# Position bias of an attention kernel: unit values in 4 bytes instead of 2-byte step tests

## The chip, the core and the metric

The kernel runs on one core of a Trainium2 chip. The metric is the time of one execution in device microseconds (us). The engines named below are TensorE (PE in the profile, its weight loads PEld), VectorE (DVE), ScalarE (ACT), GpSimd (POOL) and the queue of SyncE (SP), which issues most DMAs.

## The reference, cut to what matters

The program is attention with a position bias, then two feed-forward parts with gates. The change touches the bias alone: for each query position i, key position j and head, a network with one input x, 32 hidden units (relu) and 8 outputs.

```python
B, H, S, D = (2, 8, 576, 64); hidden = 32
psi_rel = np.log1p(np.abs(rel))                       # rel = i - j
psi_i = np.log1p(np.maximum(pos[:, None], 1.0))
x = (psi_rel / psi_i)[..., None]
h = np.maximum(x @ w1 + b1, 0.0)                      # w1 (1, 32), b1 (32)
bias = h @ w2                                         # w2 (32, 8)
scores = scores + bias.transpose(2, 0, 1)[None, :, :, :]
...
attn = exp(scores - max) / (sum + 1e-09); out = attn @ v
...
```

## The kernel before, in words

The bias is the same for both batches and depends on i and on the distance |i - j|. It is made once, ahead of the attention, and stored to DRAM (`bias_f`), from where the attention loads it tile by tile.

The work is cut into 36 steps, `g16` = 0 to 35, of 16 query positions each. A step has four *quarters*, c = 0 to 3, of four positions; the 128 partitions of a quarter's tile `s` are four positions x 32 hidden units. Only the longer side of the distances is computed: `width(g16)` columns, 576, 564, 546, ... down to 306 and up again to 576; the other side of the row is a mirror image.

For each step, `gen_s` makes the four tiles `s` (128 partitions x width). An engine makes each: the letters of `TESTS` say which (G GpSimd, A ScalarE, V VectorE). In the kernel before, a tile holds 2-byte tests: 1 or 0 (or a steep sigmoid that is 1 or 0), whether the unit is on at that distance. `bias_mm` multiplies them on TensorE. A weight tile has 32 columns (4 positions x 8 heads), and quarter c writes PSUM partitions 32c to 32c + 31, a quarter of the array's columns. There are two sums, q = 0 (the units' slopes) and q = 1 (their offsets), and each weight is split into two 2-byte parts, p = 0 and 1; the quarter c is the innermost loop:

```python
for q in range(2):
    for p in range(2):
        for sl in sls:
            for c in range(4):
                T.matmul(out=pt[32*c:32*c+32, sl, :], lhsT=wb[p][:, q, :], rhs=s_t[4*g16+c][:, sl, :], ...)
```

VectorE then reads both sums from PSUM: `bias_ev` multiplies the first by 1/psi_i and by the table of psi (tile `t`), `bias_out` adds the second (tile `bo`). `bias_store` has ScalarE write the mirror side (`bo` from `bo`, line 396 or 401) and issues the store on SP, one step late. Ahead of the steps, VectorE works out thresholds from the weights (an exponential by a series) and the split weights; ScalarE converts the first head's q and k (`qs`, `kh`, line 194) once `qk` has landed. Tiles `s` come from a pool of 12. Unit values are made two steps ahead of the step that uses them. GpSimd makes five pieces of the first head's low parts among them (line 192).

Every engine runs its own instructions in program order. After the last step the attention begins: score matmuls (`sc`, line 469), scores plus bias on VectorE (`ng`, line 486), exponentials and so on. Later, line 977 multiplies a 4-byte tile by 4-byte ones (`pc`, 72 columns, eight calls); most other matmuls use tiles declared with a reduced 4-byte type, which the trace calls f32 too.

Of the kernel before, what the change touches and what calls it, by code (L numbers as in the profile page):

```python
# [53 lines left out]
def make_body(stop=None):  # L54
    def body(tc, a):
# [21 lines left out]
        with ctx, tc.manual_schedule():  # L77
# [131 lines left out]
            with ExitStack() as bctx:  # L209
                bc = bctx.enter_context(pool("bc"))  # L210
                sp = bctx.enter_context(pool("sp", bufs=12))
                ev = bctx.enter_context(pool("ev", bufs=2, side="right"))
                pb = [bctx.enter_context(pool("pb", bufs=2, space=PSUM, side=("right", None)[q])) for q in range(2)]
                par = bc.tile([128, 2 + H + 32 + NG4 + 2 * HID + HID * H], F32, name="par")
                rr = bc.tile([128, TW], F16, name="rr")
                tab16 = bc.tile([128, TW + NG16], F32, name="tab16")
# [21 lines left out]
                MAGIC = 1.5 * 2.0 ** 23  # L241
                one = bc.tile([128, 4], F32, name="one")
                sg, kap, dn = one[:, 0:1], one[:, 1:2], one[:, 2:3]
                eu = bc.tile([128, 5, NG4], F32, name="eu")
                v, kf, f, po, pw = (eu[:, i] for i in range(5))
                thr = bc.tile([128, NG4], F32, name="thr")
                nthr = bc.tile([128, NG4], F32, name="nthr")
                rs = bc.tile([128, TW], F16, name="rs")
                big = bc.tile([128, 2 * HID + 1], F32, name="big")
                m1, m2, top = big[:, 0:HID], big[:, HID:2 * HID], big[:, 2 * HID:]  # L250
                sc = bc.tile([128, 2], F32, name="sc")
                ab = bc.tile([128, 2, H], F32, name="ab")
# [929 lines left out]
```

## Time and profile before

| | |
|---|---|
| time, median of 3 runs | 1128.23 us (1128.06 to 1130.68) |
| span of the profiled execution | 1128.2 us |
| TensorE busy | 1093.3 us (97%) |
| VectorE busy | 692.3 us (61%) |
| ScalarE busy | 497.7 us (44%) |
| GpSimd busy | 366.5 us (32%) |

The profile is one execution, whose span runs from its first to its last instruction; of its own time nothing more is shown, and it equals the median of the runs. Shares of busy time are averages over stages with different limits: the bias stage is some 5% of the span, and there the engines stand quite differently from the table.

### The profile page before, as it was taken

Reading aid. Unit: us, or ns where it says so; the run is one execution under the profiler, and the core shown is the slowest. Engines: PE = TensorE matmul, PEld = TensorE weight load, DVE = VectorE, ACT = ScalarE, POOL = GpSimd, SP = SyncE. Lnnn points to the kernel's source line nnn. Section 1 sums busy time; section 2 is a strip of 40 time slices with the busy share of each in tenths; the row PEclk is TensorE's granted clock in tenths of the full one; section 3 lists DMA queues with packets and bytes.
Section 4 is the critical chain, followed back from the end, with each engine's and each line's share of the span. In section 5 each row is a group of like instructions: output and inputs, shape, how many; then the busy total and the mean of one; then the engine's idle time right before and its main releaser. Section 6 shows DMA issues by size and latency. Waiting matters only on the chain.

```text
span 1128.2 us, 18182 instructions
## 1 busy us (share of the span) xinstructions
PE 1093.3 (97%) x7162; PEld 985.8 (87%) x7162; DVE 692.3 (61%) x1214; ACT 497.7 (44%) x903; POOL 366.5 (32%) x258
## 2 busy tenths in 40 slices
PE   6779999999999999999999999999999999999998
PEld 3369898999999989898898988989889898898986
DVE  8989999677735866364554645546455464553633
ACT  7979898433324635152341523415234152341520
POOL 6986997122214402231220312203122031220310
PEclk8899999999999999999999999999999999999999
DMA  5887764133301201020211202112021020110102
GB/s 186 266 243 253 217 188 109 40 114 113 109 20 39 76 19 48 28 75 15 62 47 29 76 11 65 48 28 75 13 63 47 28 76 14 62 48 28 57 19 85
DMA packets 36148, 88.49 MB, mean 78 GB/s; under 512 B 5535, under 2 KB 6494, under 8 KB 35166
## 3 DMA queue, kind: packets, MB, share of 16 engines
q1 hardware_dynamic: 35918, 87.03, 25.4%
q8 instruction: 56, 0.92, 0.3%
q10 hardware_dynamic: 144, 0.29, 0.1%
q14 instruction: 30, 0.25, 0.1%
HBM read 73.24 MB, written 13.28 MB: 77 GB/s over the span
## 4 chain that ended last, share of the span: by engine, by line
PE 76%; DVE 13%; issue 3%; ACT 3%; POOL 2%; DMA 2%; DVEq 0%; SPq 0%; ACTq 0%; POOLq 0%
PE d L1092 35%; PE x L1010 12%; PE y L1010 9%; PE z L1010 8%; PE o L895 3%; PE sc L469 2%; POOL s L343 2%; PE pv L607 2%; DVE ww L106 2%; PE pt L555 1%; DVE ww L111 1%; PE m L658 1%; DVE ng L486 1%; DVE ww L109 1%; PE p L368 1%
## 5 line engine op out<-in xcount | busy, mean ns | idle before, releaser
L1078 POOL TENSOR_TENSOR w2l<-w2r,w2h 128x512 fp32r<-128x512 f32 x64 | 93.6, 1463 | 477.7 <-ACT w2h L1077 469.4
L1106 DVE SCALAR_TENSOR_TENSOR acc<-d,P,acc 128x512 f32<-128x512 f32 x126 | 94.6, 751 | 224.0 <-PE d L1092 223.9
L1092 PE MATMUL d<-w2h,hh 128*128 128x512 f32 x576 | 224.9, 390 | 0.0
L1092 PE MATMUL d<-w2h,hl 128*128 128x512 f32 x576 | 224.6, 390 | 0.0
L1092 PE MATMUL d<-w2l,hh 128*128 128x512 f32 x576 | 224.4, 390 | 0.0
L1018 ACT ACTIVATE s<-x 128x576 f32<-128x576 f32 x96 | 62.5, 651 | 352.8 <-PE x L1010 349.4
L1023 ACT ACTIVATE hh<-s 128x576 fp32r<-128x576 f32 x128 | 87.9, 687 | 93.6 <-DVE s L1035 44.6
L1092 PEld LDWEIGHTS d<-w2h,hl 128*128 128x128 f32 x576 | 108.1, 188 | 23.0 <-DVE hl L1028 0.3
L1092 PEld LDWEIGHTS d<-w2l,hh 128*128 128x128 f32 x576 | 108.2, 188 | 22.0
L1092 PEld LDWEIGHTS d<-w2h,hh 128*128 128x128 f32 x576 | 108.2, 188 | 21.8
L1028 DVE SCALAR_TENSOR_TENSOR hl<-s,hh 128x576 fp32r<-128x576 f32 x128 | 102.1, 815 | 1.8 <-ACT hh L1023 1.5
L835 POOL TENSOR_TENSOR w1l<-wf,w1h 128x768 fp32r<-128x768 f32 x32 | 59.8, 1870 | 77.5 <-ACT w1h L834 67.5
L1010 PE MATMUL x<-xth,w1h 128*128 128x288 f32 x384 | 82.4, 296 | 0.5 <-ACT acc L898 0.5
L1010 PE MATMUL x<-xtl,w1h 128*128 128x288 f32 x384 | 82.2, 296 | 0.0
L1010 PE MATMUL x<-xth,w1l 128*128 128x288 f32 x384 | 82.1, 295 | 0.0
L658 PE MATMUL m<-xh,wh 128*128 128x384 f32 x216 | 73.2, 339 | 2.0 <-DVE t L786 1.9
L658 PE MATMUL m<-xh,wl 128*128 128x384 f32 x216 | 72.8, 337 | 0.7 <-POOL wl L114 0.7
L658 PE MATMUL m<-xl,wh 128*128 128x384 f32 x216 | 72.6, 336 | 0.0
L1044 DVE TENSOR_TENSOR s<-y,s 128x576 f32<-128x576 f32 x32 | 24.2, 757 | 70.4 <-ACT w1h L838 59.4
L1010 PEld LDWEIGHTS x<-xth,w1h 128*128 128x128 f32 x384 | 62.5, 189 | 1.8 <-ACT acc L898 0.7
L1010 PEld LDWEIGHTS x<-xtl,w1h 128*128 128x128 f32 x384 | 61.8, 189 | 0.0
L1010 PEld LDWEIGHTS x<-xth,w1l 128*128 128x128 f32 x384 | 61.8, 189 | 0.0
(194 smaller groups left out, 2463.5 us busy)
## 6 DMA issues: line engine op xcount, KB each, us to landing
wf<-in_moe_w SPq DMA_DIRECT2D x32, 512.0 KB, 3.6
w2r<-in_moe_w SPq DMA_DIRECT2D x64, 256.0 KB, 2.6
bias_f<-bo SPq DMA_DIRECT2D x36, 295.5 KB, 3.4
bias<-bias_f SPq DMA_DIRECT2D x32, 288.0 KB, 3.0
wr<-in_moe_w SPq DMA_DIRECT2D x18, 512.0 KB, 3.7
qk<-in_qk SPq DMA_DIRECT2D x7, 1152.0 KB, 7.3
wr<-in_moe_w_out SPq DMA_DIRECT2D x6, 512.0 KB
vr<-in_v SPq DMA_DIRECT2D x8, 320.0 KB, 6.0
```

The costliest lines, as they stand in the source:

```text
L106: lambda: V.tensor_scalar(out=f, in0=f, scalar1=2.0 ** -15, scalar2=None, op0=ALU.max),
L658: T.matmul(out=p[:, :TG], lhsT=ws[:, 128 * c:128 * c + 128], rhs=xs[:, c, TG * g:TG * g + TG], start=(c == 0 and n == 0), stop=(c == 3 and ...
L835: G.tensor_tensor(out=lo[:, 0:3], in0=t[:, 1:4], in1=raw(hi[:, 0:3]), op=ALU.subtract)
L895: T.matmul(out=p[:, :SH], lhsT=ws[:, 128 * d:128 * d + 128], rhs=xs[:, f, SH * g:SH * g + SH], start=(k == 0), stop=(k == 17))
L1010: T.matmul(out=ps[bank][:, s, :SH], lhsT=ws[:, i, c, :], rhs=xs[:, j, c, s * SH:s * SH + SH], start=(start and k == 0), stop=(k == 5), **kw)
L1018: A.activation(out=t, in_=src, func=AF.Copy)
L1023: A.activation(out=o, in_=src, func=AF.Relu)
L1028: V.scalar_tensor_tensor(out=l, in0=src, scalar=0.0, in1=raw(o), op0=ALU.max, op1=ALU.subtract)
L1044: V.tensor_tensor(out=s2, in0=y, in1=s2, op=ALU.add)
L1078: G.tensor_tensor(out=lo, in0=r, in1=raw(hi), op=ALU.subtract)
L1092: T.matmul(out=pd, lhsT=hs[:, fh, 128 * t:128 * t + 128], rhs=ws, start=(k == 0), stop=(k == 11))
L1106: V.scalar_tensor_tensor(out=acc[:, t, :], in0=pd, scalar=P[:, t, e:e + 1], in1=acc[:, t, :], op0=ALU.mult, op1=ALU.add)
```

## The change

A tile `s` now holds 4-byte values of the units themselves: ScalarE makes relu(slope x psi + b1) with a per-partition scale and bias, GpSimd and VectorE make max(slope x psi, -b1/|w1|), to which a constant is added after the sum (`cv`, one number per output row). psi is read from a 4-byte table. The weights are one 4-byte set (`wf[0]` for ScalarE's tiles, `wf[1]` for the others), so there is one sum and one matmul per quarter, in rounds of at most 512 columns. VectorE reads the sum from PSUM twice: forwards for the computed side, backwards for the mirror side, adding `cv`. ScalarE no longer mirrors. The letters are G, A, V, A in every step. Pools: 14 tiles `s`, 6 tiles `bo`. The thresholds, the series and the weight splitting are gone, as is one input table.

```diff
-TESTS0 = "VVVAAAGG"
-TESTS = "GAVA"
-TESTSL = "GAAA"
+KMAX = 16.0
+TESTS = ("GAVA",)
...
-                sp = bctx.enter_context(pool("sp", bufs=12))
-                ev = bctx.enter_context(pool("ev", bufs=2, side="right"))
+                sp = bctx.enter_context(pool("sp", bufs=14))
+                ev = bctx.enter_context(pool("ev", bufs=6, side="right"))
...
-                par = bc.tile([128, 2 + H + 32 + NG4 + 2 * HID + HID * H], F32, name="par")
-                rr = bc.tile([128, TW], F16, name="rr")
-                tab16 = bc.tile([128, TW + NG16], F32, name="tab16")
+                par = bc.tile([128, 2 + H + 32 + NG4], F32, name="par")
+                tab = bc.tile([128, TW], F32, name="tab")
                 dma(par, a["par"])
-                nc.scalar.dma_start(out=rr, in_=a["tab4"])
-                dma(tab16, a["tab16"])
+                dma(tab, a["tab"])
...
+                ts(sg, w1r, 0.0, ALU.is_ge, 2.0, ALU.mult)
+                ts(sg, sg, -1.0, ALU.add)
+                ts(sl[0], ic4, w1r, ALU.mult)
+                ts(aw, w1r, sg, ALU.mult, 1e-30, ALU.max)
+                ts(sl[1], ic4, sg, ALU.mult)
+                V.reciprocal(out=rec, in_=aw)
+                V.scalar_tensor_tensor(out=wf[0].rearrange("p (i h) -> p i h", h=H),
+                                       in0=w2r.unsqueeze(1).to_broadcast([128, 4, H]), scalar=8.0,
+                                       in1=msk.rearrange("p (i h) -> p i h", h=H), op0=ALU.mult, op1=ALU.mult)
+                ts(nk, b1r, rec, ALU.mult, -1.0, ALU.mult)
+                ts(cb, aw, -KMAX, ALU.mult, b1r, ALU.max)
+                ts(nk, nk, -KMAX, ALU.max, KMAX, ALU.min)
+                ts(wf[1], wf[0], aw, ALU.mult)
...
-                    s = sp.tile([128, 3, 194], F16, tag="s", name="s")[:, :, :n // 3]
-                    win = v3(window(rs, g // 4))
-                    kind = TESTS0[g] if g < len(TESTS0) else (TESTSL if g // 4 == NG16 - 1 else TESTS)[g % 4]
-                    if kind == "A":
-                        A.activation(out=s, in_=win, func=AF.Sigmoid, bias=nthr[:, g:g + 1], scale=STEEP)
+                    s = sp.tile([128, S + 6], F32, tag="s", name="s")
+                    out, win = s[:, :n], window(g // 4)
+                    if kind(g) == "A":
+                        A.activation(out=out, in_=win, func=AF.Relu, bias=b1r, scale=sl[0][:, g:g + 1])
                     else:
-                        eng = G if kind == "G" else V
-                        eng.tensor_scalar(out=s, in0=win, scalar1=thr[:, g:g + 1], scalar2=None, op0=ALU.is_gt)
+                        eng = G if kind(g) == "G" else V
+                        eng.tensor_scalar(out=out, in0=win, scalar1=sl[1][:, g:g + 1], scalar2=nk, op0=ALU.mult, op1=ALU.max)
...
-                    for q in range(2):
-                        pt, sls = sums(pb[q].tile([128, 2, 512], F32, tag="p", name="p"), width(g16))
-                        ps.append(pt)
-                        for p in range(2):
-                            for sl in sls:
-                                for c in range(4):
-                                    T.matmul(out=pt[32 * c:32 * c + 32, sl, :], lhsT=wb[p][:, q, :],
-                                             rhs=s_t[4 * g16 + c][:, sl, :], start=(p == 0), stop=(p == 1))
+                    n = width(g16)
+                    pt = pb[g16 % 2].tile([128, 2, 512], F32, tag="p", name="p").rearrange("p a n -> p (a n)")
+                    for j0 in range(0, n, 512):
+                        js = slice(j0, min(n, j0 + 512))
+                        for c in range(4):
+                            g = 4 * g16 + c
+                            T.matmul(out=pt[32 * c:32 * c + 32, js], lhsT=wf[kind(g) != "A"], rhs=s_t[g][:, js],
+                                     start=True, stop=True)
...
-                    V.scalar_tensor_tensor(out=v3(t), in0=ps[0], scalar=ics[:, g16:g16 + 1], in1=v3(window(l16, g16)),
-                                           op0=ALU.mult, op1=ALU.mult)
...
-                    V.scalar_tensor_tensor(out=v3(bo[:, o:o + n]), in0=ps[1], scalar=sc[:, 1:2], in1=v3(t),
-                                           op0=ALU.mult, op1=ALU.add)
...
-                        A.activation(out=bo[:, 0:z], in_=bo[:, 2 * z:z:-1], func=AF.Copy)
...
+                    for x, y in ((bo[:, at:at + n], pt[:, :n]), (to, src)):
+                        V.tensor_scalar(out=x, in0=y, scalar1=cv, scalar2=None, op0=ALU.add)
...
-                    for n in range(max(g16 - 1, 0), NG16 if g16 == NG16 - 1 else g16):
-                        bias_store(n)
+                    bias_store(g16)
```

TensorE, first step (576 columns), as it stands before: rounds of 2 x 192 and 192 columns, the quarter changing with each matmul; `wb_138` and `wb_139` are the two 2-byte parts of the weights, each matmul with a weight load ahead of it.

```order
L368 LDWEIGHTS wb_138
L368 MATMUL p<-s,wb_138 32x2x192
...
L368 LDWEIGHTS wb_138
L368 MATMUL p<-s,wb_138 32x192
...
L368 LDWEIGHTS wb_139
L368 MATMUL p<-s,wb_139 32x2x192
```

TensorE, the same step after the change: `wf_129` goes with the tiles of GpSimd and VectorE, `wf_128` with ScalarE's.

```order
L297 MATMUL p<-s,wf_129 32x512
L297 MATMUL p<-s,wf_128 32x512
L297 MATMUL p<-s,wf_129 32x512
L297 MATMUL p<-s,wf_128 32x512
L297 MATMUL p<-s,wf_129 32x64
L297 MATMUL p<-s,wf_128 32x64
L297 MATMUL p<-s,wf_129 32x64
L297 MATMUL p<-s,wf_128 32x64
```

Thirty-two matmuls of a step (16 in a step of at most 512 columns) became eight (four), one per quarter and round, each a single row that loads its own weights.

VectorE, steps 0 and 1, as they stand before: `t` and `bo` are the two reads of PSUM, `s` a unit value for a step two further on.

```order
L377 SCALAR_TENSOR_TENSOR t<-p,ics,tab_103 128x576
L343 TENSOR_SCALAR s<-rs,thr 128x3x182
L387 SCALAR_TENSOR_TENSOR bo<-p,sc,t 128x576
L377 SCALAR_TENSOR_TENSOR t<-p,ics,tab_103 128x564
L343 TENSOR_SCALAR s<-rs,thr 128x3x176
L387 SCALAR_TENSOR_TENSOR bo<-p,sc,t 128x564
```

VectorE, the same steps after the change:

```order
L276 TENSOR_SCALAR s<-tab,sl_127,one 128x546
L317 TENSOR_SCALAR bo<-p,cv 128x576
L317 TENSOR_SCALAR bo<-p,cv 128x15
L276 TENSOR_SCALAR s<-tab,sl_127,one 128x528
L317 TENSOR_SCALAR bo<-p,cv 128x564
L317 TENSOR_SCALAR bo<-p,cv 128x31
```

The first read of PSUM is gone, the unit value stands ahead of the step's reads, and the mirror side (15 and 31 columns here) has come to VectorE.

## Rows read from the trace of the kernel before

**Rows 1.** Windows by stretch: busy us of each engine, granted clock, DMA share, GB/s.

```profile
core 0: us, PE busy (x) PEld busy (x) DVE busy (x) ACT busy (x) POOL busy (x), PEclk, DMA share, GB/s
...
12.00:15.00 3.00, 3.00 (x40) 2.10 (x43) 1.76 (x4) 3.00 (x6) 3.00 (x3) 0.50 0.00 0
15.00:45.00 30.00, 23.72 (x398) 9.80 (x391) 29.94 (x63) 27.41 (x62) 29.64 (x24) 1.00 0.79 247
45.00:57.00 12.00, 8.72 (x116) 4.32 (x118) 10.49 (x23) 10.36 (x23) 12.00 (x10) 0.72 0.74 220
...
69.40:73.40 4.00, 3.97 (x17) 3.72 (x18) 3.05 (x7) 1.96 (x5) 3.83 (x3) 0.57 0.76 196
```

**Rows 2.** Chain that ended last, end of the bias stage: start us, us, what.

```profile
63.15 3.42 POOL s L343 x2
...
67.84 0.81 DVE bo L387
...
69.43 4.08 PE sc L469 x16
...
73.64 0.76 DVE ng L486
...
74.81 8.41 DMA bias<-bias_f
```

**Rows 3.** Lines grouped, first 70 us: count | busy us, mean ns | idle before, releaser.

```profile
L343 POOL TENSOR_SCALAR s<-rs,thr 128x564 f16<-128x564 f16 (+17 forms) x36 | 49.3, 1390 | 10.1 <-DVE thr L239 9.9
L340 ACT ACTIVATE s<-rs,nthr 128x576 f16<-128x576 f16 (+17 forms) x72 | 43.1, 650 | 2.0 <-PE p L368 1.6 <-DVE nthr L239 0.3
L368 PE MATMUL p<-s,wb 128*32 128x384 f16 (+21 forms) x736 | 43.0, 341 | 18.8 <-POOL s L343 11.2 <-DVE s L343 6.1 <-DVE bo L387 0.2
L387 DVE SCALAR_TENSOR_TENSOR bo<-p,sc,t 128x576 f32<-128x576 f32 (+17 forms) x36 | 24.2, 671 | 0.7 <-PE p L368 0.4 <-DVE t L377 0.2
L377 DVE SCALAR_TENSOR_TENSOR t<-p,ics,tab 128x576 f32<-128x576 f32 (+17 forms) x36 | 24.1, 670 | 2.7 <-PE p L368 2.7
...
L343 DVE TENSOR_SCALAR s<-rs,thr 128x576 f16<-128x576 f16 (+17 forms) x36 | 15.5, 435 | 0.0
```

**Rows 4.** Timeline of TensorE, one bias step of 546 columns: start us, us.

```profile
16.44 1.11 PE L368 MATMUL p<-s,wb 128*32 128x364 f16 x32 [0.34 <-POOL s L343]
```

**Rows 5.** Timeline of TensorE from 16.44 to 16.46 us.

```profile
16.44 0.34 PE L368 MATMUL p<-s,wb 128*32 128x364 f16 x4 [0.34 <-POOL s L343]
```

**Rows 6.** Timeline of TensorE, a 4-byte product behind others.

```profile
408.18 0.39 PE L1092 MATMUL d<-w2l,hh 128*128 128x512 f32 x1
408.41 0.39 PE L1092 MATMUL d<-w2h,hl 128*128 128x512 f32 x1
408.64 0.34 PE L977 MATMUL pc<-P,ones 128*128 128x72 f32 x2
```

**Rows 7.** Instructions of line 977 alone: ns min/median/max, first and last start.

```profile
L977 PE MATMUL pc<-P,ones x16: 223/248/273, 408.6 to 429.7; 128*128 128x72 f32 x16
```

**Rows 8.** Lines by shape, whole span: count | busy us, mean ns | idle before.

```profile
L1018 ACT ACTIVATE s<-x 128x576 f32<-128x576 f32 x96 | 62.5, 651 | 352.8 <-PE x L1010 349.4
...
L64 POOL TENSOR_SCALAR xh<-x 128x576 fp32r<-128x576 f32 x6 | 4.0, 675 | 0.5
...
L340 ACT ACTIVATE s<-rs,nthr 128x576 f16<-128x576 f16 x4 | 2.9, 765 | 0.3 <-DVE nthr L239 0.3
```

**Rows 9.** Timeline of ScalarE ahead of the bias stage.

```profile
8.99 1.16 ACT L194 ACTIVATE qs<-qk 128x1152 fp32r<-128x1152 f32 x1 [4.70 <-DMA qk<-in_qk]
10.06 1.15 ACT L194 ACTIVATE kh<-qk 128x1152 fp32r<-128x1152 f32 x1
```

**Rows 10.** Timeline of VectorE: end of its preparation, and the last step's `t`.

```profile
11.21 0.29 DVE L239 TENSOR_SCALAR nthr<-eu,one 128x144 f32<-128x144 f32 x1
...
68.57 0.81 DVE L377 SCALAR_TENSOR_TENSOR t<-p,ics,tab 128x576 f32<-128x576 f32 x1
```

**Rows 11.** DMA rate from 0 to 15 us, in 40 slices.

```profile
GB/s 0 0 0 0 54 76 79 257 375 418 429 424 418 454 510 393 418 418 418 418 548 270 396 294 55 0 0 0 0 0 0 0 0 0 0 0 0 0 0 0
```

More of the change, by code (lines that the diff above doesn't have):

```diff
@@ L239, in ts @@
                     V.tensor_scalar(out=out, in0=in0, scalar1=s1, scalar2=s2, op0=o0, **kw)
[L241 to L252, printed above, removed]
-                wf = bc.tile([128, 2, 32], F32, name="wf")
-                wb = [bc.tile([128, 2, 32], F16, name=f"wb{p}") for p in range(2)]
-                ics = bc.tile([128, NG16], F32, name="ics")
@@ L299, in body @@
-                weights += [lambda q=q: V.tensor_tensor(
-                    out=wf[:, q, :].rearrange("p (i h) -> p i h", h=H),
-                    in0=ab[:, q, :].unsqueeze(1).to_broadcast([128, 4, H]),
-                    in1=msk.rearrange("p (i h) -> p i h", h=H), op=ALU.mult) for q in range(2)]
-                weights += [
-                    lambda: V.tensor_copy(out=wb[0], in_=wf),
-                    lambda: V.tensor_tensor(out=wb[1], in0=wf, in1=wb[0], op=ALU.subtract),
-                    lambda: ts(ics, ic16, sc[:, 1:2], ALU.mult)]
@@ L308, in body @@
-                weights.insert(10, lambda: ts(pw.bitcast(I32), kf, 127.0, ALU.add, 2.0 ** 23, ALU.mult))
-                for n in range(max(len(knots), len(weights))):
-                    for steps in (knots, weights):
-                        if n < len(steps):
-                            steps[n]()
-                    if n == 4:
-                        ts(rs, rr, sg, ALU.mult)
+                one = bc.tile([128, 8], F32, name="one")
+                sg, aw, rec, nk, cb = (one[:, i:i + 1] for i in range(5))
@@ new lines, in body @@
+                sl = [bc.tile([128, NG4], F32, name=f"sl{i}") for i in range(2)]
+                wf = [bc.tile([128, 32], F32, name=f"wf{i}") for i in range(2)]
+                cv = bc.tile([128, 1], F32, name="cv")
+                V.memset(cv, 0.0)
+                ts(sg, w1r, 0.0, ALU.is_ge, 2.0, ALU.mult)
[3 more added lines that the diff above has]
+                ts(sl[1], ic4, sg, ALU.mult)
@@ L351, in body @@
                     gen_s(g)
[L353 to L369 removed]
+                for c in range(4):
+                    T.matmul(out=p0[32 * c:32 * c + 32, 0, 0:1], lhsT=wf[0], rhs=cb, start=True, stop=True)
@@ new lines, in body @@
+                for c in (0, 2):
+                    V.tensor_copy(out=cv[32 * c:32 * c + 32], in_=p0[32 * c:32 * c + 32, 0, 0:1])
+                def bias_mm(g16):
+                    n = width(g16)
+                    pt = pb[g16 % 2].tile([128, 2, 512], F32, tag="p", name="p").rearrange("p a n -> p (a n)")
+                    for j0 in range(0, n, 512):
+                        js = slice(j0, min(n, j0 + 512))
+                        for c in range(4):
+                            g = 4 * g16 + c
+                            T.matmul(out=pt[32 * c:32 * c + 32, js], lhsT=wf[kind(g) != "A"], rhs=s_t[g][:, js],
+                                     start=True, stop=True)
@@ L381, in body @@
[L381 to L402 removed]
+                    i0 = 16 * g16
@@ L408, in body @@
[L408 removed]
+                    pt = bias_mm(g16)
                     for c in range(4):
```

106 lines of the change are left out of this document (22 added, 84 removed).

## The prediction, made before the changed kernel ran

> **What bounds the kernel now.** I read the windows by stretch first, then the chain that ended last, then the grouped lines of the bias stage, then single TensorE rows. In the windows [rows 1] the reader is to see that the position bias fills the time from 12 to about 69.4 us, with GpSimd busy 12.0 of 12.0 us in its worst stretch and VectorE 29.9 of 30.0 in its longest, while TensorE has gaps: its granted clock stands at 0.50 (1.2 GHz) when the stage starts, rises to 1.00 (2.4 GHz), and averages 0.72 between 45 and 57 us and 0.57 just after the stage. The chain [rows 2] ends the stage with GpSimd's unit values (line 343), one short TensorE piece, VectorE's sum into `bo`, and the first score matmul at 69.43; from there it goes through `ng` at 73.64 and a bias load of 8.41 us. Everything later is a TensorE-bound program that the change doesn't touch, so what counts is when the first score matmul and the first `ng` start. The grouped lines [rows 3] give the load of the 36 steps: GpSimd 49.3 us of unit values, ScalarE 43.1 us of unit values, VectorE 24.1 + 24.2 us of evacuation and 15.5 us of unit values.
>
> **The change, part by part.** Widths n of the 36 steps go 576, 564, 546, 528, 516, 498, ... 306 and back up; their sum is 15912, their mean 442.
>
> *GpSimd.* The same 36 unit values, now 4 bytes in and out, two operations. The nearest row is a 4-byte two-operation copy of 576 columns at 0.675 us [rows 8]; the 2-byte test of 564 columns is the longest form behind the mean of 1.390 [rows 3]. From below 36 x 0.56 = 20 us (0.675 less 134 columns at 0.86 ns, the slope of a line through a small fixed cost), from above the 49.3 us it costs now. I take 20, since type and kind of the copy are those of the new operation. Hidden in either case unless TensorE's part below comes out under 50 us.
>
> *ScalarE.* 72 Relu in place of 72 Sigmoid, at one element rate; each gets a second per-partition operand. An ACTIVATE without one took 0.651 us at 576 columns, the present one with one 0.765 [rows 8], so a second is worth 0 to 0.11 us: 43.1 + 72 x (0 to 0.11) = 43 to 51 us, taken as 47. The mirror copies leave it.
>
> *VectorE.* `t` goes (24.1 us). `bo` stays at the same price per column, since its operand is still PSUM (24.2 us), and a mirror piece of 15 to 287 columns, 151 on average, comes in: 36 x (0.2 + 151 x 1.06 ns) = 13 us, rate and fixed cost from the present sums (0.81 us at 576 columns, mean 0.670 at 442 [rows 3, 10]). Unit values 15.5 us, or up to 24 at the rate of the sums. Together 53 to 61 us against 63.8 now, all of these durations, of which neighbours overlap a little. Under TensorE's part, and in step with it.
>
> *The prelude.* VectorE's preparation (some 40 operations; the last starts at 11.21 [rows 10]) becomes 12 small ones, so GpSimd and VectorE can start near 6.5 instead of 11.4. ScalarE can't: it first makes the two head copies, which waited for `qk` until 8.99 [rows 9]. The input is smaller by 0.47 MB of the 2.29 MB that land up to then (`rr` gone, `par` 93 instead of 253 KB); at the 0.42 MB/us at which the queues ran [rows 11] that is 1.1 us. Copies from 7.9 to 10.1, the first Relu done at about 11.0. Before, TensorE's first bias matmul stood at 11.98.
>
> *TensorE.* This is the step on which the forecast rests. Now, 2-byte operands: at n = 546 the 32 matmuls of a step took 1.11 us [rows 4]. Each column quarter sees 2 x 2 x 546 = 2184 columns, 0.91 us at 2.4 GHz, plus the tail of the last one, so all four quarters run at once; a stretch of 20 ns holds the starts of four, and no fifth, which would go to the first quarter again [rows 5]. After: one 4-byte matmul per quarter. The only true 4-byte products in the trace are `pc` (72 columns): eight calls left sixteen matmul records [rows 7], so each is two passes. Two passes from 408.64 to their end took 0.34 us [rows 6]; the second took 0.273 [rows 7], so it began 0.06 to 0.07 us after the first: 72 columns at two clocks each (0.06 us). The neighbouring `d` rows move 512 columns in 0.23 us, one clock each. So a quarter needs 4n clocks in two passes, as many as the 2-byte form's 4n in four passes.
>
> But the order of the passes differs. In the old order the quarter changes with every matmul. In the new one both passes of a quarter stand back to back, and the second can't start while the first occupies the same quarter. If TensorE starts matmuls in program order, then the next quarter's first pass starts only together with this quarter's second: two quarters at a time, not four. A step with n up to 512 costs 4 x 2n clocks = 3.33n ns. For n above 512 the code makes a round of 512 columns over four quarters and then a round of n - 512; the short round hides behind the last long pass, but that pass no longer covers the next step's first: 5 x 0.427 + 2(n - 512)/2.4 ns = 2.14 to 2.19 us. Sum: the 26 steps up to 498 (10452 columns) 34.8 us, the ten wide ones 21.6 us, 56.4 us. That is longer than ScalarE's 47, and makes TensorE the bound of the stage.
>
> The Trainium skill says in "TensorE: Matmul & The Clock Gate", Part 3 (What overlaps and what doesn't), that matmuls start and end strictly in program order. By that rule the step costs what I have just worked out; no row here has two passes on one quarter followed by another quarter, so the trace doesn't show it.
>
> *Sum.* 11.0 (first unit of ScalarE) + 56.4 + 0.8 (some 165 passes in series, 5 ns between them, an estimate from the 0.06 to 0.07 above) + 1.6 (the clock stood at 0.50 for about 3.2 us from the first bias matmul [rows 1], half of which is lost) = 69.8 for the last bias matmul and the first score matmul behind it, against 69.43: +0.4. The first `ng` waits for VectorE too, which has the last `bo` (0.81) and its mirror (0.2) to make after TensorE's last pass and its tail (0.16, a `pc` pass of 0.223 us less its 72 columns): 1.2 us, where it now starts about a quarter of the 4.08 us of score matmuls behind the first. That adds 0.2. Coming back: without gaps TensorE should enter the scores at full clock. Now those sixteen matmuls ran at a mean clock of 0.57 and the chain goes through them to the fourth `ng` [rows 1, 2]; four `ng` of 0.76 behind each other are then the longer part, and some 0.5 us are won. Net 0 to +0.6 us. The profiled execution's span is 1128.2 us and the runs' median 1128.23, so no correction is needed: 1128.7.
>
> **The rivals.**
>
> *Four quarters at once* (faster). If the two passes of different quarters interleave freely, TensorE needs 4n clocks a step, 27 us in all, and ScalarE sets the pace: 10.1 + 47 + 0.7 (the value copy) = 58, first score at 59, 10.4 us earlier: about 1118. For it: the 2-byte rows show four quarters at once. Against it: they are in an order that asks for nothing else. The Trainium skill's table in the same page ("Why this matters for your kernels") promises concurrency for small outputs on separate column groups without a word on operand size. By that advice this rival holds.
>
> *One quarter at a time* (slower). If 4-byte passes on different quarters don't overlap at all, a step takes 8 x 2n clocks = 6.67n ns, 106 us in all, the first score comes near 119 and the kernel at 1178. It decides from the first step. Nothing in the trace shows 4-byte passes on two quarters together; nothing speaks against it but that 2-byte ones do.
>
> *Two quarters at the low clock* (slower). If TensorE isn't given 1.00 with half its columns working, 56 us become 113: 1183. Against it: between 15 and 45 us it kept 1.00 although it was busy only 23.7 of 30 us with tails counted [rows 1].
>
> *The new unit values don't get cheaper on GpSimd.* 49 us plus its 10 us of head pieces from 6.5 on ends at 66, a few steps late behind the pieces: 1131 or 1132, within the likeliest case's range.
>
> **How the numbers follow.** Two quarters at full clock 0.70, four 0.10, one 0.10, low clock 0.08, something else 0.02. The likeliest gives 1128.7; its own range is 1125 to 1133: 1.5 us either way for the start of ScalarE and the clock, up to 2.6 us if 20 ns instead of 5 lie between passes, 3 if GpSimd stays dear. What a measurement tells from no change here is 0.3%, 3.4 us. Inside the likeliest case 0.50 is no change, 0.07 faster, 0.13 slower. Faster: 0.10 + 0.07 = 0.17; same 0.50; slower 0.13 + 0.10 + 0.08 + 0.02 = 0.33. The two slow cases are 0.18 together and stay outside the range; the four-quarter case is taken in: 1117 to 1134.
>
> **What would show it.** Right: in the profile after, TensorE without gaps from about 11 to 70 us; two matmul records per quarter; starts of passes of 512 columns 0.43 us apart in pairs; 2.1 to 2.2 us per step at the wide end and 1.0 at 306; GpSimd at 0.55 us per unit value and waiting for buffers; clock 1.00 at the first score matmul. Wrong: starts within some 10 ns for four quarters, and a stage that ends near 58 with ScalarE full; or steps of 3.8 us at 576 and a stage that ends near 119; or a clock of 0.50 through the stage. If ScalarE's Relu took over 0.9 us at 576, or GpSimd over 1.7, one of them would be the bound instead of TensorE.

## The result, and the profile after

The changed kernel takes 1142.04 us, median of four runs (1139.98 to 1143.22), against 1128.24 (1128.06 to 1130.68) for the kernel before: ratio 1.0113, 95% interval 1.0099 to 1.0128. It is 13.8 us slower, outside the range of 1117 to 1134. The profiled execution's span is 1141.4 us, 13.2 more than that of the kernel before; it is the longest of the four runs.

The windows by stretch of the changed kernel, for the stretches of [rows 1] and the 4 us behind its bias stage:

```profile
core 0: us, PE busy (x) PEld busy (x) DVE busy (x) ACT busy (x) POOL busy (x), PEclk, DMA share, GB/s
12.00:15.00 3.00, 3.00 (x24) 1.46 (x24) 0.53 (x1) 3.00 (x5) 3.00 (x2) 0.50 0.00 0
15.00:45.00 30.00, 20.67 (x166) 4.85 (x162) 25.61 (x54) 23.94 (x38) 29.62 (x19) 0.76 0.76 231
45.00:57.00 12.00, 8.45 (x56) 1.23 (x52) 8.10 (x18) 7.66 (x12) 12.00 (x8) 0.57 0.59 165
80.90:84.90 4.00, 3.50 (x31) 3.12 (x24) 3.59 (x9) 1.73 (x5) 3.92 (x3) 1.00 0.70 176
```

GpSimd is the full engine now, 29.6 of 30 and 12.0 of 12 us, and VectorE, which had 29.94 of 30 [rows 1], has room. TensorE is busy less than before, and its granted clock is lower, 0.76 between 15 and 45 us, where it was 1.00. The lines grouped over the first 84 us (count | busy us, mean ns | idle before, releaser) say what it waits for:

```profile
L276 POOL TENSOR_SCALAR s<-tab,sl,one 128x576 f32<-128x576 f32 (+17 forms) x36 | 68.1, 1901 | 4.5 <-DMA tab<-in_tab 4.3
L273 ACT ACTIVATE s<-tab,par,sl 128x576 f32<-128x576 f32 (+17 forms) x72 | 49.2, 746 | 14.9 <-PE p L297 14.9
L297 PE MATMUL p<-s,wf 128*32 128x512 f32 (+18 forms) x368 | 48.4, 608 | 26.3 <-POOL s L276 24.6 <-ACT s L273 1.2
L317 DVE TENSOR_SCALAR bo<-p,cv 128x576 f32<-128x576 f32 (+17 forms) x72 | 34.5, 521 | 21.5 <-PE p L297 21.5
L276 DVE TENSOR_SCALAR s<-tab,sl,one 128x576 f32<-128x576 f32 (+17 forms) x36 | 23.9, 666 | 1.4 <-DMA tab<-in_tab 1.4
```

These answer to [rows 3]. TensorE waits 24.6 us for GpSimd's unit values. The 36 of them take 68.1 us, 1.90 us each, where the tests took 1.39 [rows 3] and the forecast was 0.55. By shape:

```profile
L276 POOL TENSOR_SCALAR s<-tab,sl,one 128x576 f32<-128x576 f32 x2 | 5.0, 2514 | 4.3 <-DMA tab<-in_tab 4.3
...
L273 ACT ACTIVATE s<-tab,par,sl 128x576 f32<-128x576 f32 x4 | 3.3, 856 | 0.5 <-PE p L297 0.5
```

The chain that ended last (start us, us, what), from the last head piece to the first wait for a bias load, answers to [rows 2]:

```profile
57.86 1.39 POOL kl L190
59.25 10.91 POOL s L276 x6
...
73.09 6.69 POOL s L276 x3
...
79.82 1.22 PE p L297 x16
...
81.80 0.24 DVE bo L317
...
82.06 3.40 DMA bias_f<-bo
...
86.10 9.20 DMA bias<-bias_f
```

The end of the stage is GpSimd's, with TensorE's sixteen passes behind it. GpSimd's own timeline has no gap over 0.1 us from its first unit value to its last; the first and the last row of unit values:

```profile
5.77 28.27 POOL L276 TENSOR_SCALAR s<-tab,sl,one 128x576 f32<-128x576 f32 x14 [4.29 <-DMA tab<-in_tab]
...
59.23 20.54 POOL L276 TENSOR_SCALAR s<-tab,sl,one 128x432 f32<-128x432 f32 x10
```

From 5.77 us on, 68.1 us of unit values and four head pieces of 1.4 us (the last is `kl` at 57.86) add up to 79.5; the last value ends at 79.77. The first score matmul stands at 80.93 instead of 69.43 [rows 2], 11.5 us later. The bias load behind it starts 11.3 us later than the one in [rows 2] and takes 9.20 instead of 8.41 us. Line 977 of the kernel before, now line 895, starts at 422.4 instead of 408.6 [rows 7], 13.8 us later, so the whole loss lies ahead of it:

```profile
L895 PE MATMUL pc<-P,ones x16: 223/248/273, 422.4 to 443.4; 128*128 128x72 f32 x16
```

Of the 13.8 us, 12.1 are there when that load has landed (95.30 against 83.22); the other 1.7 fall between there and line 895, and I have not followed them.

The timeline of TensorE (start us, us, idle before) holds the second surprise. The first two rows are the same step of 480 columns, up to 21.46 us and up to 21.90 us; the others are the last step and the first three scores:

```profile
21.43 0.61 PE L297 MATMUL p<-s,wf 128*32 128x480 f32 x4 [0.90 <-POOL s L276]
...
21.43 1.02 PE L297 MATMUL p<-s,wf 128*32 128x480 f32 x8 [0.90 <-POOL s L276]
...
79.82 1.18 PE L297 MATMUL p<-s,wf 128*32 128x512 f32 x16 [1.10 <-POOL s L276]
80.93 0.40 PE L387 MATMUL sc<-kh,qs 128*128 128x288 f32 x1
81.17 0.29 PE L387 MATMUL sc<-kl,qs 128*128 128x288 f32 x1
81.30 0.29 PE L387 MATMUL sc<-kh,qs 128*128 128x288 f32 x1
```

A 4-byte matmul is two passes (two records each, as in [rows 7]), so the step has eight. Four of them start within 30 ns; the other four start after 21.46 and before 21.90 (a pass of 480 columns at two clocks each takes 0.40 us), and all eight are done in 1.02 us with the tail. The forecast's order, two at a time, gives 1.6 us and the tail. So four run at once, which I take for the first passes of the four quarters. The last step, 576 columns, took 1.18 us; 2.19 were forecast.

### The profile page after: what moved, and what is told of

It reads as the page before. It is cut to its first block, busy times and chain, and to the rows that moved or that the text cites. A ratio compares the mean times of both kernels' runs of the same rounds, so it can differ in the third digit from the quotient of the medians.

```text
span 1141.4 us, 17296 instructions
## 1 busy us (share of the span) xinstructions
PE 1098.8 (96%) x6802; PEld 976.0 (86%) x6802; DVE 685.3 (60%) x1187; ACT 493.5 (43%) x864; POOL 384.7 (34%) x258
## 4 chain that ended last, share of the span: by engine, by line
PE 74%; DVE 12%; POOL 5%; issue 3%; ACT 3%; DMA 2%; SPq 0%; DVEq 0%; ACTq 0%; POOLq 0%
PE d L1010 34%; PE x L928 12%; PE y L928 8%; PE z L928 8%; POOL s L276 4%; PE o L813 3%; PE sc L387 2%; PE pv L525 2%; DVE ww L104 2%; PE pt L473 2%; DVE ww L109 1%; PE m L576 1%; DVE ng L404 1%; DVE ww L107 1%; DVE ptl L487 1%
## 5 line engine op out<-in xcount | busy, mean ns | idle before, releaser
L297 PE MATMUL p<-s,wf 128*32 128x512 f32 (+18 forms) x368 | 48.4, 608 | 26.3 <-POOL s L276 24.6
L276 POOL TENSOR_SCALAR s<-tab,sl,one 128x576 f32<-128x576 f32 (+17 forms) x36 | 68.1, 1901 | 4.5 <-DMA tab<-in_tab 4.3
L297 PEld LDWEIGHTS p<-s,wf 128*32 128x32 f32 x368 | 11.0, 125 | 63.6 <-POOL s L276 54.3
```

Of the source, the lines that this page charges most:

```text
L276: eng.tensor_scalar(out=out, in0=win, scalar1=sl[1][:, g:g + 1], scalar2=nk, op0=ALU.mult, op1=ALU.max)
L297: T.matmul(out=pt[32 * c:32 * c + 32, js], lhsT=wf[kind(g) != "A"], rhs=s_t[g][:, js], start=True, stop=True)
```

## The experiments

**The theories.** B, as the expectations call it: GpSimd is the bound because of max. A comparing operation is dear there, a multiplication or an addition isn't. Against it stood the second per-partition operand of the new operation (A), VectorE's work beside it (C), and the 4 bytes. e4, e7, e8, e11 and e12 make the whole computation; the others leave out or change the part named. All kernels but e6 start from the changed kernel, some by way of e7; the kernel before ran beside them on the same chip (1128.35 for the first four, 1128.55 for the next four, 1128.60 and 1129.11 for the last). "First score" is the start of the first score matmul. e2 to e6, e9 and e10 ran once each, so their times have no interval, and the argument goes by the durations in their traces.

| run | GpSimd's 36 (or fewer) operations | mean us | first score | time us |
|---|---|---|---|---|
| kernel before | 2-byte is_gt | 1.39 | 69.43 | 1128.24 |
| changed kernel | 4-byte mult, max | 1.90 | 80.93 | 1142.04 |
| e1 | 4-byte mult, mult | 0.73 | 64.85 | 1124.04 |
| e2 | mult, max with a constant | 1.83 | 78.19 | 1136.66 |
| e3 | mult, add | 0.81 | 65.45 | 1125.70 |
| e4 | mult, max; VectorE makes none | 1.84 | 82.01 | 1140.00 |
| e5 | 4-byte is_gt alone | 1.50 | 67.23 | 1128.54 |
| e6 | the kernel before, 2-byte mult, mult | 0.63 | 69.10 | 1128.07 |
| e9 | 4-byte max alone | 1.50 | 67.86 | 1128.34 |
| e7 | none (mirror copies) | | 66.00 | 1124.64 |
| e8 | 18 mult, max (and mirror copies) | 1.95 | 72.66 | 1132.69 |
| e11 | 9 mult, max (and mirror copies) | 1.88 | 69.54 | 1129.68 |
| e12 | 9 mult, max, issued earlier (and mirror copies) | 2.06 | 62.20 | 1120.86 |
| e10 | none (mirror copies); 140 of 144 unit values left out | | 52.96 | 1112.64 |

**e1: no max on GpSimd.** The maximum is left out on GpSimd's quarter.

```diff
-eng = G if kind(g) == "G" else V
-eng.tensor_scalar(out=out, in0=win, scalar1=sl[1][:, g:g + 1], scalar2=nk, op0=ALU.mult, op1=ALU.max)
+if kind(g) == "G":
+    G.tensor_scalar(out=out, in0=win, scalar1=sl[1][:, g:g + 1], scalar2=1.0, op0=ALU.mult, op1=ALU.mult)
+else:
+    V.tensor_scalar(out=out, in0=win, scalar1=sl[1][:, g:g + 1], scalar2=nk, op0=ALU.mult, op1=ALU.max)
```

> GpSimd's 36 unit values are made as slope x psi x 1.0 (one per-partition operand, one constant); the max with the knee is left out on GpSimd alone, all else is as in the change. This is the form whose price the prediction used. If the price hangs on the operation (either theory, the second operand or the max), GpSimd's unit values fall from 68.1 us to 20 to 25 us (0.56 to 0.7 each, as the copies of this width), TensorE waits for something else, and the stage ends where ScalarE (49 us from 10.7) or VectorE (58 us) ends: first score matmul at 61 to 70 us instead of 80.9, time 1120 to 1129. If it is VectorE's use of the shared memory path, the form hardly matters: GpSimd stays over 55 us and the time near 1138 to 1142.

Measured: 1124.04 us (1121.93 to 1125.38, 6 runs), ratio to the kernel before 0.9957 (0.9945 to 0.9970). Lines over the first 84 us, and the window from 30 to 45 us:

```profile
L299 PE MATMUL p<-s,wf 128*32 128x512 f32 (+16 forms) x368 | 42.4, 482 | 15.4 <-DVE s L278 11.2 <-ACT s L273 3.7
...
L276 POOL TENSOR_SCALAR s<-tab,sl 128x576 f32<-128x576 f32 (+17 forms) x36 | 26.2, 730 | 23.6 <-PE p L299 19.3 <-DMA tab<-in_tab 4.0
L278 DVE TENSOR_SCALAR s<-tab,sl,one 128x576 f32<-128x576 f32 (+17 forms) x36 | 24.4, 681 | 1.2 <-DMA tab<-in_tab 1.1
```

```profile
30.00:45.00 15.00, 9.01 (x86) 2.68 (x86) 15.00 (x32) 14.52 (x25) 11.49 (x14) 1.00 0.85 266
```

GpSimd falls from 68.1 to 26.2 us and now waits for TensorE. The stage ends 16.1 us earlier, and VectorE, busy 15.00 of 15 us, is the bound: TensorE waits 11.2 us for VectorE's unit values. The two multiplications, at 26.2 us, are a little over the 20 to 25 expected and near the 20 of the forecast; what is left to 68.1 goes with max or with the second per-partition operand, which this edit takes out together.

**e2 and e3: the second per-partition operand apart from max.** In e2 max compares with a constant, in e3 the operand stays and is added, on GpSimd's quarter alone.

```diff
+    G.tensor_scalar(..., scalar2=0.0, op0=ALU.mult, op1=ALU.max)   # e2
+    G.tensor_scalar(..., scalar2=nk, op0=ALU.mult, op1=ALU.add)    # e3
```

> GpSimd's unit values are max(slope x psi, 0.0): the knee as a constant in place of the per-partition one, which changes the bias of those units. Theory A, the second per-partition operand is dear: falls to 20 to 30 us in all, as in the mult-mult kernel. Theory B, the max is dear: stays at 60 to 68 us (1.7 to 1.9 each). Theory C, VectorE's traffic: stays at 60 to 68 as well, but then the mult-mult kernel does too.

> GpSimd's unit values are slope x psi + knee: both operands per partition, but an add in place of the max, so no relu on those units. Theory A, the second per-partition operand is dear: stays at 60 to 68 us. Theory B, the max is dear: falls to 20 to 30 us. Theory C: stays.

Measured, the same line in either:

```profile
L276 POOL TENSOR_SCALAR s<-tab,sl 128x576 f32<-128x576 f32 (+17 forms) x36 | 65.3, 1830 | 4.4 <-DMA tab<-in_tab 4.3
```

```profile
L276 POOL TENSOR_SCALAR s<-tab,sl,one 128x576 f32<-128x576 f32 (+17 forms) x36 | 29.1, 810 | 21.3 <-PE p L299 16.8 <-DMA tab<-in_tab 4.2
```

Max with a constant is as dear as with an operand (1.83 against 1.90), and an addition with that operand costs 0.08 us more than a multiplication with a constant (0.81 against 0.73). The rival of the operand (A) falls: 0.07 or 0.08 us of the 1.90 are its share.

**e4: VectorE makes no unit values.** ScalarE makes three of four; the whole computation.

```diff
-TESTS = ("GAVA",)
+TESTS = ("GAAA",)
```

> VectorE's quarter is made by ScalarE (letters G, A, A, A); same results. VectorE then reads PSUM alone and makes no unit values from SBUF, so nothing of its fast reads from SBUF meets GpSimd. Theory C, VectorE's traffic makes GpSimd slow: GpSimd's 36 values fall from 1.90 us each to about 1.0 or less. Theories A and B, the form is dear by itself: they stay at 1.7 to 1.9 (only the long ones, such as 2.75 us for the first of 576 columns beside three VectorE values, come down to the straight line through the others, 2.3). ScalarE becomes the bound: 108 values, 74 us from 10.7, stage end near 86.

Measured, lines over 84 us:

```profile
L276 POOL TENSOR_SCALAR s<-tab,sl,one 128x576 f32<-128x576 f32 (+17 forms) x36 | 65.8, 1837 | 5.1 <-DMA tab<-in_tab 4.1 <-ACT s L273 0.6 <-PE p L297 0.2
...
L273 ACT ACTIVATE s<-tab,par,sl 128x576 f32<-128x576 f32 (+17 forms) x108 | 70.0, 749 | 0.0
```

GpSimd's values take 1.84 instead of 1.90 us: VectorE's unit values beside it are worth 3%. VectorE's sums, which read PSUM, still ran; in e1 both stood beside GpSimd, and its operations took 0.73 us, so C falls. ScalarE, at 70.0 us of work, is full as well (15.00 of 15 us between 30 and 45 us), so the time itself tells nothing.

**e5, e6 and e9: bytes and operation crossed.** e5 keeps only a compare on GpSimd's quarter, e9 only the maximum; e6 is the kernel before with a multiplication in place of its 2-byte test.

```diff
+    G.tensor_scalar(out=out, in0=win, scalar1=sl[1][:, g:g + 1], scalar2=None, op0=ALU.is_gt)   # e5
+    G.tensor_scalar(out=out, in0=win, scalar1=nk, scalar2=None, op0=ALU.max)                    # e9
+    G.tensor_scalar(out=s, in0=win, scalar1=sg, scalar2=1.0, op0=ALU.mult, op1=ALU.mult)        # e6
```

> GpSimd's 36 operations are a single is_gt against one per-partition value, 4 bytes in and out (slope and clamp are left out on GpSimd's quarter; the rest is the kernel after). Theory B (comparing operations are dear on GpSimd, multiplying and adding ones are not, whatever the bytes): as dear as the 2-byte test of the kernel before or dearer, 1.4 to 1.9 us mean, the first score matmul at 70 to 80 us and the kernel at 1129 to 1142. Rival (only max is dear, and the test of the kernel before was slow because of its 2 bytes): 0.7 to 0.8 us mean, first score matmul near 65, kernel near 1124.

> GpSimd's 36 operations are a single max with one per-partition value (the multiplication by the slope is left out on GpSimd's quarter; the rest is the kernel after). A multiplication alone in 4 bytes took GpSimd 0.73 us as a pair of two factors. If the two operations of one instruction cost the sum of their own prices, max alone is 1.90 less 0.4 to 0.7: 1.2 to 1.5 us mean, as the lone compare's 1.50, the first score matmul near 67, the kernel near 1128.5. If the price of max is paid once for the instruction whatever stands beside it, 1.8 to 1.9 us, and the kernel stays at 1137 to 1142.

> The kernel before, with GpSimd's 36 2-byte tests replaced by a 2-byte multiplication of two factors (the test is left out on GpSimd's tiles; all else as before). Theory B: 0.7 to 0.9 us mean instead of 1.39, 25 to 32 us in all; the stage is then set by VectorE (63.8 us of work from 6 to 12 us on, 29.9 of 30 us busy before), so the first score matmul comes 0 to 3 us earlier than 69.4 and the kernel is at 1125 to 1128. Rival (bytes make it slow): 1.3 to 1.4 us mean, and nothing changes: 1128.

Measured, GpSimd's line in e5, e9 and e6, and a window of e6:

```profile
L276 POOL TENSOR_SCALAR s<-tab,sl 128x576 f32<-128x576 f32 (+17 forms) x36 | 53.4, 1498 | 5.3 <-DMA tab<-in_tab 3.7 <-PE p L299 1.4
```

```profile
L276 POOL TENSOR_SCALAR s<-tab,one 128x576 f32<-128x576 f32 (+17 forms) x36 | 53.3, 1496 | 6.0 <-DMA tab<-in_tab 4.0 <-PE p L299 1.7
```

```profile
L343 POOL TENSOR_SCALAR s<-rs,one 128x564 f16<-128x564 f16 (+17 forms) x36 | 22.7, 634 | 33.1 <-PE p L370 19.6 <-DVE t L379 7.6 <-DVE rs L239 5.1
```

```profile
30.00:45.00 15.00, 14.29 (x184) 3.79 (x185) 15.00 (x35) 14.46 (x34) 10.51 (x15) 1.00 0.88 282
```

A lone compare and a lone maximum cost the same in 4 bytes, 1.50 us; the compare in 2 bytes cost 1.39 [rows 3]; multiplications cost 0.73 in 4 bytes and 0.63 in 2. The operation decides, the bytes count for some 10%. The prices look as if they add up: 1.50 for max leaves 1.90 - 1.50 = 0.40 for the multiplication ahead of it, about half of 0.73 for two; a lone multiplication was not run. The price of e5 came as theory B had it, but the time didn't: its first score was expected at 70 to 80 us and stands at 67.23. In e6 GpSimd's load is more than halved, to 22.7 us (25 to 32 were expected), and the kernel stays at 1128.07, against 1128.55 beside it: in the kernel before, GpSimd alone was not the bound, although it stood in the chain at the end of the stage [rows 2]. VectorE is full in that window of e6, 15.00 of 15 us, with ScalarE at 14.46 and TensorE at 14.29 close to it.

**e10: TensorE by itself.** From e7 (below); only the first step's four unit values are made, and all steps multiply those.

```diff
-for g in range(8):
+for g in range(4):
     gen_s(g)
...
-    T.matmul(..., rhs=s_t[g][:, js], start=True, stop=True)
+    T.matmul(..., rhs=s_t[c][:, js], start=True, stop=True)
...
-    for c in range(4):
-        if g16 + 2 < NG16:
-            gen_s(4 * (g16 + 2) + c)
```

> The kernel of the run without a max on GpSimd, in which only the first step's four unit values are made; all 36 steps multiply those (the other 140 unit values are left out). TensorE then waits for no value, only for the sum buffers, which VectorE frees in 24 us in all. Two quarters at a time in program order, as forecast: 2.1 to 2.2 us for a step of 516 to 576 columns, 1.0 us for one of 306, 56 us for all steps from about 11.5 on, the last near 68. Four quarters at once: 0.95 to 1.1 us for a wide step, 0.55 to 0.65 for one of 306, 27 to 32 us in all at 2.4 GHz, the last step near 40 to 45.

Measured: weight loads on TensorE come in fours, one for each quarter, two fours to a step. The timeline of the loads of the steps of 468 (two fours), 450 (two) and 432 columns (the first four, in a row with what follows), at full clock, and the lines of TensorE and VectorE:

```profile
19.35 0.19 PEld L297 LDWEIGHTS p<-s,wf 128*32 128x32 f32 x4 [0.21 <-issue]
19.75 0.20 PEld L297 LDWEIGHTS p<-s,wf 128*32 128x32 f32 x4 [0.20 <-DVE bo L317]
20.14 0.20 PEld L297 LDWEIGHTS p<-s,wf 128*32 128x32 f32 x4 [0.19 <-issue]
20.52 0.22 PEld L297 LDWEIGHTS p<-s,wf 128*32 128x32 f32 x4 [0.17 <-DVE bo L317]
20.89 0.97 PEld L297 LDWEIGHTS p<-s,wf 128*32 128x32 f32 x12 [0.16 <-issue]
```

```profile
L297 PE MATMUL p<-s,wf 128*32 128x512 f32 (+18 forms) x368 | 35.8, 525 | 9.2 <-DVE bo L317 5.8 <-ACT s L273 3.4
L317 DVE TENSOR_SCALAR bo<-p,cv 128x576 f32<-128x576 f32 (+17 forms) x36 | 24.4, 678 | 24.1 <-DMA bias_f<-bo 12.1 <-PE p L297 10.0 <-POOL bo L62 0.5
```

From 19.35 to 20.14 the step of 468 columns takes 0.79 us, from there to 20.89 that of 450 takes 0.75: 4n clocks at 2.4 GHz are 0.78 and 0.75 us. Four quarters at once, without a remainder. So TensorE needs about 27 us for the 15912 columns at 2.4 GHz, not 56. The last step was expected near 40 to 45, but from 24 us on VectorE waits 12.1 us for stores to free `bo`, and the first score stands at 52.96: with nearly no unit values made, the stores hold the stage there.

**e7: a version without max on GpSimd.** The whole computation. VectorE makes two of four unit values, and GpSimd copies the mirror side from the finished `bo`.

```diff
-TESTS = ("GAVA",)
+TESTS = ("VAVA",)
...
+def msrc(bo, m, n, up_):
+    return bo[:, 2 * m:m:-1] if up_ else bo[:, n - 2:n - 2 - m:-1]
...
-for x, y in ((bo[:, at:at + n], pt[:, :n]), (to, src)):
-    V.tensor_scalar(out=x, in0=y, scalar1=cv, scalar2=None, op0=ALU.add)
+V.tensor_scalar(out=bo[:, at:at + n], in0=pt[:, :n], scalar1=cv, scalar2=None, op0=ALU.add)
+pool_copy(to, msrc(bo, m, n, side(g16)[1]))
```

> The whole computation: GpSimd makes no unit values, VectorE makes two of four, and GpSimd makes the mirror piece of the sum by a 4-byte copy from the finished part. GpSimd: 36 copies of 151 columns on average at 0.2 to 0.35 us, 7 to 13 us, no max. VectorE: 36 sums at 0.67 us, 24 us, and 72 unit values at 0.35 us (the short ones of the kernel after) to 0.68 us (its mean beside GpSimd), 25 to 49 us: 49 to 73 us from 5.7 on. ScalarE: 72 Relu at 0.68 us, 49 us from 10.6 on. Theory B with VectorE little disturbed: the stage ends by ScalarE or VectorE at 58 to 64, first score matmul at 60 to 66 instead of 80.9, kernel at 1119 to 1125, faster than both. Rival (VectorE's unit values stay at 0.68 us even without GpSimd's): VectorE ends near 78, kernel near 1138.

Measured: 1124.64 us (1123.84 to 1125.15, 4 runs), ratio 0.9963 (0.9948 to 0.9977).

```profile
L276 DVE TENSOR_SCALAR s<-tab,sl,one 128x576 f32<-128x576 f32 (+17 forms) x72 | 36.9, 556 | 1.3 <-DMA tab<-in_tab 1.3
L319 DVE TENSOR_SCALAR bo<-p,cv 128x576 f32<-128x576 f32 (+17 forms) x36 | 23.8, 666 | 5.5 <-PE p L297 5.3
L62 POOL TENSOR_SCALAR bo<-bo 128x15 f32<-128x15 f32 (+17 forms) x36 | 17.7, 492 | 41.9 <-DVE bo L319 40.9 <-ACT s L273 0.8
```

The upper end of what was expected: VectorE has 60.7 us, unit values at 0.56 us. The 36 mirror copies cost GpSimd 0.49 us each, more than the 0.2 to 0.35 expected, but GpSimd waits 40.9 us for VectorE's sums ahead of them. 17.4 us of the changed kernel are gone.

**e8, e11, e12: some max on GpSimd.** The whole computation, from e7. GpSimd makes one value in every second step (e8), in every fourth (e11), or in every fourth but issued four steps ahead of its use instead of two, with 16 tiles `s` instead of 14 (e12). In e11 and e12 alike the values are issued at steps 1, 5, 9 and so on up to 29, and the head pieces at others; only one value of the nine is placed differently, at step 33 for the last step in e11, ahead of the first step in e12.

```diff
+TESTS = ("GAVA", "VAVA")                   # e8
+TESTS = ("VAVA", "VAVA", "VAVA", "GAVA")   # e11
+TESTS = ("VAVA", "GAVA", "VAVA", "VAVA")   # e12
...
+sp = bctx.enter_context(pool("sp", bufs=16))                     # e12
...
-        if g16 + 2 < NG16:
+        if g16 + 2 < NG16 and kind(4 * (g16 + 2) + c) != "G":    # e12
             gen_s(4 * (g16 + 2) + c)
+    if g16 + 4 < NG16 and kind(4 * (g16 + 4)) == "G":
+        gen_s(4 * (g16 + 4))
```

> The whole computation, as the run beside it, but GpSimd makes its unit value (with max) in every second step: 18 values at 1.85 us, 33 us, plus 7 to 13 us of mirror copies and about 10 us of head pieces: 50 to 56 us from 5.7 on, so it ends at 56 to 62. VectorE: 36 sums, 24 us, and 54 unit values at 0.35 to 0.68 us, 19 to 37 us: 43 to 61 us. ScalarE as in the kernel after, 49 us from 10.6 on, ends at 60. If the price of a max is all that made the kernel after slow, all three end near 60 and the first score matmul is at 60 to 64: 1119 to 1123. If GpSimd's long operations hold up its mirror copies, which the stores wait for, the gain is less: 64 to 72, 1123 to 1131.

> The whole computation; as the run without a max on GpSimd, but in every fourth step GpSimd makes one unit value: 9 values at 1.9 us, issued two steps before a head piece and two after, so that each has two steps of about 1.5 us. VectorE has 9 unit values of 0.56 us less: 55.7 us instead of 60.7, and it was busy all the time from 15 to 60 us. If GpSimd's long operations fit between the pieces, the first score matmul comes 2 to 5 us earlier than 66.0, at 61 to 64, the kernel at 1120 to 1123. If TensorE again waits for GpSimd, as with a max in every second step, it comes at 66 to 69: 1124 to 1128.

> The whole computation; GpSimd makes one unit value with a max in every fourth step, as in the run before, but issues it four steps ahead of its use instead of two, at a step that has no head piece and not for the wide last step (a pool of 16 tiles s instead of 14). If TensorE's waits of 2 us for each of the nine values came from GpSimd's queue (the value stands behind a mirror copy, which waits for the sum of the step before), they go, VectorE keeps its 5 us of relief, and the first score matmul comes at 61 to 65 instead of 69.5: kernel at 1120 to 1124. If they came from GpSimd's load or from disturbance of VectorE by GpSimd's long operations, it stays at 67 to 70: 1126 to 1130.

Measured: e8 1132.69 us (1130.74 to 1133.07, 6 runs), ratio 1.0033 (1.0020 to 1.0045); e11 1129.68 (1127.97 to 1131.65, 12 runs), 1.0006 (0.9998 to 1.0015); e12 1120.86 (1118.94 to 1122.18, 5 runs), 0.9928 (0.9915 to 0.9942). e8 and e11 came out just beyond even the slower case expected of them (64 to 72 us and 1123 to 1131 us, 66 to 69 and 1124 to 1128), e12 within the faster one. TensorE's line in e8, its timeline from 20 to 38 us in e11 with two rows of GpSimd's, and the lines of e12:

```profile
L297 PE MATMUL p<-s,wf 128*32 128x512 f32 (+18 forms) x368 | 41.0, 570 | 24.7 <-POOL s L276 22.7 <-ACT s L273 2.0
```

```profile
24.54 3.67 PE L297 MATMUL p<-s,wf 128*32 128x468 f32 x32 [2.13 <-POOL s L276]
30.19 3.36 PE L297 MATMUL p<-s,wf 128*32 128x402 f32 x32 [1.98 <-POOL s L276]
35.98 2.39 PE L297 MATMUL p<-s,wf 128*32 128x336 f32 x20 [2.44 <-POOL s L276]
...
22.10 0.48 POOL L62 TENSOR_SCALAR bo<-bo 128x79 f32<-128x79 f32 x1 [1.07 <-DVE bo L319]
22.57 1.91 POOL L276 TENSOR_SCALAR s<-tab,sl,one 128x468 f32<-128x468 f32 x1
```

```profile
L273 ACT ACTIVATE s<-tab,par,sl 128x576 f32<-128x576 f32 (+17 forms) x72 | 47.1, 743 | 0.4 <-PE p L297 0.3
L297 PE MATMUL p<-s,wf 128*32 128x512 f32 (+17 forms) x368 | 46.1, 481 | 9.7 <-DVE s L276 4.3 <-ACT s L273 3.7 <-PE p L297 0.5
L276 DVE TENSOR_SCALAR s<-tab,sl,one 128x576 f32<-128x576 f32 (+17 forms) x63 | 33.0, 559 | 0.8 <-DMA tab<-in_tab 0.8
...
L276 POOL TENSOR_SCALAR s<-tab,sl,one 128x564 f32<-128x564 f32 (+8 forms) x9 | 18.5, 2056 | 3.7 <-DMA tab<-in_tab 3.7
```

In e11 TensorE stands 2 us for each of GpSimd's values, 19.0 us for all nine, although GpSimd has only 16.9 us of them. A value stands in GpSimd's queue behind the mirror copy of an earlier step, which waits for VectorE's sum (22.10); the value then takes 1.91 us to 24.48, and TensorE's step starts at 24.54. So GpSimd can't run ahead of TensorE as it does in the changed kernel, and a value with max doesn't fit into what is left of two steps. Issued four steps ahead, the values cost TensorE no wait that the line of e12 still names, though GpSimd spends more time on them, 18.5 us. The two further tiles and the one value that moved were changed together with the distance; their share is not shown, but one value in nine can't be the 19.0 us.

## Why the prediction was wrong, point by point

- **GpSimd.** This step failed, and it made the time. "I take 20, since type and kind of the copy are those of the new operation": the copy is of multiplications, the new operation contains a maximum. Measured 68.1 us, beyond the upper bound of 49.3 too. The nearest row was the compare itself, 1.39 us, which the prediction used for its upper bound only because it was the work removed (e5, e9: same price for is_gt and max). And it was no upper bound, since the multiplication ahead of the maximum comes on top, 0.40 us (e9 against the changed kernel). From the rows at hand, 1.39 plus half of the 0.56 us for two multiplications is 1.67, 60 us in all: less than measured, but longer than TensorE's 56. In the Trainium skill, "GPSIMD Engine Reference", section 4.1 (Engine selection), a one-input add, multiplication or maximum on GpSimd is put at about line rate, without a difference between them; the runs agree for the first two (0.73 and 0.81 us at 442 columns; in e1 0.60 us at 306 columns and 0.89 at 576, some 1.07 ns for a column, where the prediction has VectorE's sums at 1.06), not for max (1.50; in e9 1.13 and 1.86 us, some 2.7 ns for a column).
- **TensorE.** This step failed as well, towards the other side, and hid behind the first. Passes of all four quarters run together (e10: 0.79 us for 468 columns), 27 us in all instead of 56.4. The rule of the Trainium skill cited for it, in "TensorE: Matmul & The Clock Gate", Part 3 (What overlaps and what doesn't), speaks of matmuls; I applied it to the two passes inside one, and by that reading the step of 468 columns would take 1.56 us. The times of e10 leave no room for the second pass of a matmul to hold up another quarter's first. The table of the same page under "Why this matters for your kernels" is borne out here, for 4-byte operands too (0.79 us, all four quarters).
- **The rival "Four quarters at once"** had the right mechanism, but its time of 1118 left out the next engine. With GpSimd made cheap (e1) the stage ends at 64.85, not 59, because VectorE is full, and the kernel is at 1124. The forecast gave this mechanism 0.10 and the two-quarter one 0.70.
- **The rival on GpSimd** named the place that decided, at the price of 49 us. Put 68.1 there, with 5.8 for the start and 5.7 for the four head pieces that fall into the stage, and its own sum gives 79.6 for the last value, measured at 79.77. It had no chance of its own, and no case above 49 us. The limit stated at the end of the forecast (GpSimd over 1.7 us at 576 columns: the bound) was passed at 2.51.
- **ScalarE**: 49.2 us, in 43 to 51 (taken as 47). At 576 columns its unit value takes 0.09 us more (0.856 against 0.765 [rows 8]); function and type changed together with the second per-partition operand, so the operand's own share isn't shown. **VectorE**: 34.5 + 23.9 = 58.4 us, in 53 to 61. Both right, and off the path in the changed kernel. **The prelude**: GpSimd at 5.77 where 6.5 was forecast, so nothing was lost there.
- **The clock**: the scores run at full clock, 1.00 between 80.9 and 84.9 us, from the second on 0.13 us apart, as forecast, but not for the reason given. The forecast had no gaps ahead of them; TensorE waited 1.10 us ahead of the last step alone. The clock averaged 0.76 between 15 and 45 us and 0.57 between 45 and 57, and was back at 1.00 from 66.9 to 80.9.
- **Two readings** in the prediction are off, without weight for the outcome. The five head pieces take 7.2 us together in the trace of the kernel before, not 10. The longest of GpSimd's tests has 576 columns (1.74 us), not 564.

## What to carry to other kernels

Price an operation by a row with the same arithmetic, not by one with the same shape and type: on GpSimd a compare or a maximum cost twice as much as two multiplications, and the row that said so was that of the work taken out. When one engine is costed as the bound by an argument and not by a row, ask what the next engine would do if the argument fell: here the next was GpSimd, and behind it VectorE. And a long operation on an engine that also waits for the others is issued well ahead of its use or not at all: with nine values on GpSimd the kernel took 1.0006 of the time of the kernel before when they were issued two steps ahead, 0.9928 when four ahead with two more tiles, and 0.9963 with none at all.

## What the runs showed of the hardware that was not expected

- GpSimd, 4 bytes, 128 partitions, 442 columns on average: multiplication twice 0.73 us, multiplication and addition 0.81, is_gt 1.50, max 1.50, multiplication and max 1.83 to 1.90; in 2 bytes 0.63 for two multiplications and 1.39 for is_gt. From 306 to 576 columns multiplication twice goes from 0.60 to 0.89 us (e1), max alone from 1.13 to 1.86 (e9), multiplication and max from 1.53 to 2.51 (changed kernel).
- 4-byte matmuls of two passes on four column quarters run side by side, at two clocks for a column and a pass: 0.79 and 0.75 us for steps of 468 and 450 columns (e10).
- TensorE's granted clock, a mean over its two levels, was 0.57 between 45 and 57 us of the changed kernel, where its records filled 8.45 of 12 us, and 1.00 in e1 between 30 and 45 us, where they filled 9.01 of 15.
